# Two norm tiles transposed by transfers, and a filter transposed by column-tiled products, in a fused mixer kernel

## The chip, the cores and the metric

The kernel runs on one core of a Trainium2 chip. The core's engines run side by side: TensorE (PE in the profile, with PEld for its weight loads), VectorE (DVE), ScalarE (ACT), GpSimd (POOL) and SyncE (SP), which here issues nearly all transfers (DMAs). The metric is the device time of one execution in microseconds; of a kernel, the median over its executions.

## The reference

Rows are 2048 tokens of 640 channels; all inputs are bfloat16. The result is `g*a + (1-g)*b`, with `g = sigmoid(sum(q*gate_w))` for each token.

- Branch a: `k` passes through a causal filter of 4 taps, `kv = k_shift * v`, and `kv` is convolved along the tokens with a filter of 2048 taps per channel (`ssm_k`), by Fourier transforms of length 4096; then `y + kv*ssm_D`, times `q`.
- Branch b, a mixer: `h = gelu(layernorm(x) @ w1)`, the four quarters of whose channels are shifted by 1, -1, 2 and -2 tokens, then `x1 = x + shifted @ w2`, and `x1 + gelu(layernorm(x1) @ w3) @ w4`, with `x = q`.

## The kernel before

The tokens lie in 16 *slots* of 128 (`s` below, one partition for each token). The convolution is done as a Fourier transform written as matrix products, in four steps. Step 1 (`s1h` for the filter, `s1x` for `kv`) multiplies each slot's 128x640 block by cosines and sines (`TRIG`), step 2 (`s2h`, `s2x`) transforms along the slots, `pa`/`pb` multiply the two spectra on VectorE, `s3` and `s4` transform back. Between the steps the data go to DRAM and come back in another layout: `wF` writes step 1's result, `rF` reads it, `wG` and `rG` do the same behind `s3`.

Names used below, with their lines in the profile: `st1`, `rs1`, `nm1` are statistics and normalisation of the first layer norm (L577 to L631); `tr1` transposes two normalised slots on TensorE (L609) and `ev1`/`evh` copy them from PSUM to `xnT` (L387 on ScalarE, L389 on VectorE; `evh` makes the two wrapped-around slots at either end). `w1` is the product with w1 (L689, L693 for its 32-column tail), `w2` that with w2 (L715), `x1` adds it to x (L722). `w3`, `w4` (L817, L833, L842) are the second half of the mixer. `kv` (L878, L882, L886) is the chain of 32 VectorE operations for `k_shift * v`. `fo` (L1051) writes the last output rows.

The filter comes in channel-major (`SK`, 128 channels x 2048 taps, five blocks) and must be turned to tap-major (`HT`). `trh` (L859) does one block by 16 TensorE transposes of 128x128, whose stationary operand is every 16th tap of `SK`, into one bf16 PSUM pair of banks; `evt` copies the 128x2048 result out. That puts the two token halves `g` on alternating partitions, so step 1 of the filter (L911) contracts over all 128 partitions with a matrix `BM` in which every other row is zero: `BM` is cleared by GpSimd (`bz`, L499) and filled by two transfers from `TRIG` (`bm`, L503). Step 1 of `kv` (L913) has the halves in partitions 0 to 63 and 64 to 127, and multiplies each half in its own 64x128 tile of TensorE.

The order of all work is a list of task numbers, `ORDER`, each with a letter for its engine; every engine does its tasks in that order, whatever is ready. A planner (`Plan.place`) walks the list with a duration for each task and fixes which buffer each task takes. It also decides how many *fill* products (L255: products of a zero tile with no use, to keep TensorE running while it waits in the first microseconds) stand in front of each task. The fills read the zero tile `FZ`, which the task `zeros` (L506) clears on VectorE. Semaphores come from the real dependences; the planner's times do not enter the program.

TensorE's order before, up to step 2 (cN.. are groups of four slots; a mode other than 128x128 in brackets):

```
fill gwm trh.1 sgm tr1.4 trh.2 trh.4 tr1.0 trh.3 tr1.2 tr1.14 w1.0.3 w1.0.0 w1.0.2 w1.0.1 trh.0 w1.1.2
s1h.4 s1hr.4 tr1.6 s1h.0 w1.0.4[128x32] tr1.8 w1.1.0 s1h.7 s1h.6 s1h.5 w1.1.1 w1.1.4[128x32] s1hr.0 s1h.3
w1.1.3 w2.3 w2.1 s1h.1 w2.2 w2.0 w2.4 s1h.2 tr1.10 w2.6 s1h.8 s1h.10 w2.5 s1h.11 w2.7 tr1.12 w1.2.2 s1hr.8
s1h.9 w1.2.0 s1h.12 w1.2.4[128x32] w1.2.3 s1h.15 s1h.13 w1.3.2 w1.3.1 s1hr.12 w1.3.3 s1h.14 w1.2.1 w1.3.4[128x32]
w1.3.0 w2.10 w2.9 (then s1x[64x128] in eleven runs among w2, gate and w3.0) s1x.1 s1x.3 w4.2 w4.1 w4.0 w4.3
s2h.0.0 ...
```

36 fills are issued: 5 before `fill`, 6 before `gwm`, 14 before `tr1.4`, 11 in the gaps behind. On SP stand in order, from the 11th on: `ldsk3 ldw1 ldx6 ldsk0 bm ldx10 wCJ ldk15 ldk11 rCJ ldw2b3 ldw2a ldw2b1 ldw2b0 ldw2b2 ldkh1 wFh.4 ldk7 ldv3 ldk3 wFh.0 ldw3 ldkh0 ldv2 wFh.8.1 dt2.0`. `ldkN` and `rCJ` bring `k` and the four taps, without which `kv` can't start; `dt2` are transfers that transpose the second norm's rows. `wCJ` writes out the taps that GpSimd has rearranged (`cjp`). No more than eight transfers are in flight: the ninth waits for the first.

Of the kernel before, what the change touches and what calls it, by code (L numbers as in the profile page):

```python
# [83 lines left out]
class Plan:  # L84
# [13 lines left out]
    def add(self, name, eng, dur, fn, r=(), w=(), use=(), acq=(), rel=(), roles=(), after=(), mode=None, nbytes=0):  # L98
# [3 lines left out]
        t.kept = None  # L102
        t.acq = [(a, 1, a == "U") if isinstance(a, str) else a for a in acq]
# [13 lines left out]

    def close(self):
        by_role = {}
# [27 lines left out]
    def place(self, order):  # L147
# [6 lines left out]
        mode, bw, flying, self.kept = None, 0.0, [], None  # L154
        start, end = [None] * n, [None] * n
        for i in order:
# [34 lines left out]
            else:  # L191
                d = t.dur
# [17 lines left out]
                free[e] = end[i] = at + d  # L210
            for (o, p, k) in t.rel:
# [143 lines left out]
def build(env, nc, io):  # L355
    pl = Plan()
    add = pl.add
    for name, n in (("U", 8), ("xn", 4), ("hs", 2), ("x1nT0", 1), ("x1nT1", 1), ("h2", 2), ("FS", 2), ("FX", 5), ("XS", 2), ("HS", 2), ("PP", 2),
                    ("GX", 4), ("Q", 2), ("O", 2), ("V", 4)):
        pl.pool(name, n)  # L360
# [50 lines left out]
    add("ident", "POOL", 0.55, c_id, r=["iotb"], w=["ID"])  # L411
# [86 lines left out]
    BM = lambda: env.early("BM", [P, 2, 2048], BF16)  # L498
    add("bz", "POOL", 1.9, lambda t: nc.gpsimd.memset(BM().rearrange("p g q -> p (g q)").bitcast(F32), 0.0), r=["ID"], w=["BM"], roles=("C0",))  # L499
# [4 lines left out]
    add("bm", "SP", 1.08, c_bm, r=["TRIG"], w=["BM"], nbytes=P * 4096 * HALF, roles=("C0",))  # L504

# [6 lines left out]
    add("cjp", {"POOL": 3.2, "ACT": 2.3}, 0, lambda t: copy(t, env["VC"][0:1, 3, :, :],  # L512
# [104 lines left out]
    DMA1 = ()  # L617
    pairs = [2, 4, 6, 8, 0, 14, 10, 12]
    for s0 in pairs:
        nm = []  # L620
        for s in (s0, s0 + 1):
            st1[s] = add(f"st1.{s}", {"DVE": 1.26, "ACT": 1.73}, 0, lambda t, s=s: f_st1(t, s), r=[("x", s, 0), ("x", s, 1)],
                         w=[("MV", s)])
            add(f"rs1.{s}", "POOL", 0.85, lambda t, s=s: f_rs1(t, s), r=[("MV", s), "c0"], w=[("RS", s)])
        for s in (s0, s0 + 1):
# [7 lines left out]
            nm1[s] = add(f"nm1.{s}", {"DVE": 0.445, "ACT": 1.2}, 0, f_nm1, r=[("RS", s), ("x", s, 0), ("x", s, 1)],  # L633
# [10 lines left out]
        def f_ev1(t, s0=s0, tt=tt):  # L644
            copy(t, env["xnT"][:, s0 + 2:s0 + 4, :, :], tview(env.Ub(tt.buf["U"][0])))
        add(f"ev1.{s0}", {"ACT": 1.25, "DVE": 0.82}, 0, f_ev1, use=[tt], rel=[(tt, "U")], w=[("xnT", s0), ("xnT", s0 + 1)],
            roles=("xnT",))
        if s0 in (14, 0):
            h0 = 0 if s0 == 14 else 18

            def f_evh(t, s0=s0, tt=tt, h0=h0):
# [10 lines left out]
            add(f"evh.{s0}", {"DVE": 1.0, "ACT": 1.3}, 0, f_evh, use=[tt], rel=[(tt, "U")], w=[("xnT", a), ("xnT", a + 1)],  # L662
                roles=("xnT",))
# [130 lines left out]
    for c in range(4):  # L794
        nT, nP = None, f"x1nT{c % 2}"
        for s0 in (4 * c, 4 * c + 2):
            ss = (s0, s0 + 1)
            add(f"ve2.{s0}", {"DVE": 0.42, "POOL": 1.5}, 0, lambda t, s0=s0: f_ve2(t, s0), r=[("x", s, 0) for s in ss] + [("S2", s) for s in ss],
# [308 lines left out]
```

## Time and profile before

| | us |
|---|---|
| median of 3 executions (224.55 to 225.7) | 225.08 |
| the profiled execution, its own time | 227.05 |
| its span, first to last event | 225.3 |
| TensorE busy | 212.7 |
| VectorE busy | 189.3 |
| ScalarE busy | 154.4 |
| GpSimd busy | 45.8 |

Busy time counts fills as well as work. Rows of windows give, for one stretch, its length, then the busy time of each engine with its number of instructions in brackets (PE, PEld, DVE, ACT, POOL), the granted TensorE clock (1.00 is full speed, and it was that throughout), the share of the 16 DMA engines that were busy, and GB/s. Rows of the chain give start, length and the work; rows of a timeline give start, length, engine, line, operation, tiles and count, and in square brackets the idle time before it and what ended it.

### The profile page before, as it was taken

The page shows a single profiled execution, that of the slowest core. Times are in us where ns is not written, and L with a number is a line of the kernel's source. Part 1 is how long each engine was busy: PE and PEld are TensorE (multiplying, and loading weights), DVE is VectorE, ACT ScalarE, POOL GpSimd, SP SyncE. Part 2 cuts the span into 40 slices and gives each one's busy share as a digit, 9 for nine tenths or more (in the row PEclk, how much of TensorE's full clock was granted, in tenths as well). Part 3 has the DMA queues.
Part 4 walks back from the last instruction along what each step waited for, and adds up shares of the span by engine and source line. Part 5 has one row for each costly group of instructions (what it writes and reads, how often), then busy time and mean ns, then how long its engine had stood idle before and what let it go on. Part 6 is the DMA issues. An engine that isn't in the chain of part 4 may idle for free.

```text
span 225.3 us, 5381 instructions
## 1 busy us (share of the span) xinstructions
PE 212.7 (94%) x2161; PEld 106.4 (47%) x2178; DVE 189.3 (84%) x281; ACT 154.4 (69%) x225; POOL 45.8 (20%) x86
## 2 busy tenths in 40 slices
PE   3999889899999999999999999999999999999992
PEld 1576454466444444345543433334444555555561
DVE  7998896999999999997469989899857426989984
ACT  6998969799988999889658988888675002225000
POOL 7481532436200009930710000000000000000000
PEclk9999999999999999999999999999999999999999
DMA  6999999999999998979899989999992596988624
GB/s 193 281 308 232 220 237 238 327 233 327 349 240 287 241 272 252 379 270 270 193 367 311 373 154 285 316 304 309 247 255 88 185 374 209 281 250 249 203 64 116
DMA packets 39503, 57.94 MB, mean 257 GB/s; under 512 B 15027, under 2 KB 30645, under 8 KB 39478
## 3 DMA queue, kind: packets, MB, share of 16 engines
q1 hardware_dynamic: 39158, 57.27, 89.9%
q10 hardware_dynamic: 320, 0.33, 0.5%
q8 instruction: 17, 0.28, 0.5%
q14 instruction: 8, 0.07, 0.1%
HBM read 35.56 MB, written 18.36 MB: 239 GB/s over the span
## 4 chain that ended last, share of the span: by engine, by line
PE 63%; DMA 17%; DVE 12%; SPq 3%; issue 2%; ACT 1%; DVEq 0%
PE PS L817 18%; PE PS L833 17%; PE PS L715 9%; DMA x<-in_A_q_dram 7%; PE PS L965 5%; DMA W<-in_B_w_dram 4%; PE PS L689 4%; PE PS L993 4%; DMA SK<-in_A_ssm_k_dram 3%; DVE VC L878 3%; DVE VC L882 3%; DMA QO<-in_A_q_dram 2%; SPq L382 2%; PE PS L911 2%; PE PS L1031 1%
## 5 line engine op out<-in xcount | busy, mean ns | idle before, releaser
L824 ACT ACTIVATE h2T<-PS 128x512 bf16<-128x512 f32 x48 | 27.9, 605 | 27.3 <-PE PS L817 26.9
L833 PE MATMUL PS<-W,h2T 128*128 128x512 bf16 (+3 forms) x306 | 39.8, 298 | 0.3
L387 ACT CAST FS<-PS 128x1024 bf16<-128x1024 f32 x37 | 36.0, 1021 | 5.4 <-PE PS L913 3.5
L817 PEld LDWEIGHTS <-W 128*128 128x128 bf16 (+1 forms) x300 | 22.1, 103 | 29.4 <-issue 8.4
L833 PEld LDWEIGHTS <-h2T 128*128 128x128 bf16 (+1 forms) x312 | 22.4, 100 | 18.5 <-issue 1.6
L387 ACT CAST XH<-PS 128x1024 bf16<-128x1024 f32 x26 | 25.5, 1020 | 7.5 <-PE PS L965 7.4
L817 PE MATMUL PS<-x1nT,W 128*128 128x512 bf16 x120 | 28.5, 380 | 0.0
L817 PE MATMUL PS<-XB,W 128*64 128x512 bf16 (+1 forms) x180 | 28.5, 380 | 0.0
L980 DVE TENSOR_TENSOR PP<-XH 128x2048 bf16<-128x2048 bf16 x20 | 23.6, 1219 | 3.1 <-ACT XH L387 2.8
L878 DVE TENSOR_TENSOR VC<-K,VC 128x2560 bf16<-128x2560 bf16 x16 | 23.7, 1490 | 2.3 <-DMA W<-in_B_w_dram 2.1
L715 PE MATMUL PS<-W,hsT 128*128 128x128 bf16 (+1 forms) x155 | 23.5, 297 | 0.9 <-DMA W<-in_B_w_dram 0.6
L850 DVE TENSOR_TENSOR x<-PS,x 128x640 bf16<-128x640 f32 x12 | 9.8, 823 | 13.4 <-PE PS L833 13.2
L689 PE MATMUL PS<-xnT,W 128*128 128x512 bf16 x80 | 19.2, 379 | 0.1
L715 PEld LDWEIGHTS <-hsT 128*128 128x128 bf16 x160 | 12.8, 98 | 13.0 <-issue 1.1
L882 DVE TENSOR_TENSOR VC<-VC 128x2560 bf16<-128x2560 bf16 x12 | 17.9, 1489 | 0.3
L389 DVE CAST XH<-PS 128x1024 bf16<-128x1024 f32 x14 | 16.9, 1220 | 1.2 <-PE PS L965 1.1
L1037 DVE SCALAR_TENSOR_TENSOR W<-PS,GG,QO 128x640 bf16<-128x640 f32 x16 | 13.6, 877 | 2.4 <-PE PS L1031 1.9
L387 ACT CAST GS<-PS 128x1024 bf16<-128x1024 f32 x12 | 12.0, 1016 | 3.9 <-PE PS L993 3.9
L255 PE MATMUL PS<-C 128*128 128x512 bf16 x34 | 9.9, 434 | 3.8 <-DVE C L506 3.7
L842 PE MATMUL PS<-W,h2T 128*64 128x512 bf16 (+1 forms) x192 | 13.4, 299 | 0.0
L722 DVE SCALAR_TENSOR_TENSOR x<-PS,x 128x640 bf16<-128x640 f32 x16 | 12.8, 815 | 0.1
L965 PE MATMUL PS<-FX,TRIG 64*32 64x512 bf16 x320 | 12.4, 381 | 0.3 <-ACT GS L387 0.3
(115 smaller groups left out, 294.0 us busy)
## 6 DMA issues: line engine op xcount, KB each, us to landing
FH<-FS SPq DMA_DIRECT2D x8, 640.0 KB, 6.3
FXD<-FS SPq DMA_DIRECT2D x8, 640.0 KB, 5.0
FX<-FH SPq DMA_DIRECT2D x10, 512.0 KB, 6.0
FX<-FXD SPq DMA_DIRECT2D x10, 512.0 KB, 5.3
GX<-GD SPq DMA_DIRECT2D x8, 640.0 KB, 5.9
W<-in_B_w_dram SPq DMA_DIRECT2D x2, 1920.0 KB, 11.9
GD<-GS SPq DMA_DIRECT2D x8, 480.0 KB, 4.0
SK<-in_A_ssm_k_dram SPq DMA_DIRECT2D x5, 512.0 KB, 6.5
```

Of the source, the lines that this page charges most:

```text
L387: nc.scalar.copy(out=out, in_=in_)
L389: (nc.vector if t.on == "DVE" else nc.gpsimd).tensor_copy(out=out, in_=in_)
L689: nc.tensor.matmul(m[:, b, :], lhsT=W[:, 0, kb, 160 * fb:160 * fb + 128], rhs=rhs(kb, shifts[fb]), start=(kb == 0), stop=(kb == 4))
L715: nc.tensor.matmul(m[:, c0:c1], lhsT=env["hsT"][:, o.buf["hs"][0], fb, 128 * (s % 4):128 * (s % 4) + 128], rhs=env["W12"][:, 1, fb, c0:c1] ...
L817: nc.tensor.matmul(env.PS[q:q + w, t.buf["U"][0], :], lhsT=env["W3"][:, kb, 128 * fb + q:128 * fb + q + w], rhs=env.nT(int(nP[-1]))[:, :, ...
L824: nc.scalar.activation(out=env["h2T"][:, o.buf["h2"][0], fb, :], in_=env.PS[:, t.buf["U"][0], :], func=ACT.Gelu_apprx_tanh)
L833: nc.tensor.matmul(m[q:q + w, c0:c1], lhsT=env["h2T"][:, o.buf["h2"][0], fb, a:a + w], rhs=env["W4"][:, fb, c0:c1], start=(fb == 0), stop= ...
L878: nc.vector.tensor_tensor(out=VC[:, o], in0=env["K"][:, a + 3 - j:a + 7 - j, :], in1=w, op=ALU.mult)
L882: nc.vector.tensor_tensor(out=VC[:, 1], in0=VC[:, 1], in1=VC[:, 2], op=ALU.add)
L965: nc.tensor.matmul(env.U(t.buf["U"][0])[32 * j:32 * j + 32, gp, :], lhsT=CRI()[64 * gp:64 * gp + 64, 32 * pc:32 * pc + 32], rhs=X[64 * gp: ...
L980: nc.vector.tensor_tensor(out=env["PP"][:, o.buf["PP"][0], a, :].rearrange("p (b c) -> p b c", b=2), in0=X.unsqueeze(1).broadcast_to([P, 2 ...
L1037: nc.vector.scalar_tensor_tensor(out=u, in0=env.Uf(t.buf["U"][0])[:, 0:D], scalar=SS("GG")[:, s:s + 1], in1=env["QO"][:, 2 * q.buf["Q"][0] ...
```

## The change

1. **Slots 10 to 13 of the first norm.** `tr1.10`, `tr1.12` and their copies `ev1.10`, `ev1.12` go. Four transposing transfers `dt1.10` to `dt1.13`, issued by SP, bring the rows from `xn` to `xnT`.
2. **The filter's transposes.** Each of five blocks of 16 transposes becomes two tasks of 16 plain products with the identity, in 128x64 tiles: the stationary operand is 64 columns of `SK`, taps 32 apart, for one half `g`; the result is f32, so one pair of banks holds half a block. The ten copies `evt.cb.h` take 128x1024 each. The halves now lie in partitions 0 to 63 and 64 to 127.
3. **The filter's step 1** uses the same 64x128 products as `kv`'s. `BM`, the clearing `bz` and the transfers `bm` go.
4. **A new order, new durations and new rules for the planner.** Its durations for several small tasks are changed; it now models VectorE operations that wait for two GpSimd tasks, and keeps `ev1` and `evh` of slots 0 and 14 from running at once. None of these is an instruction of its own. All of `ORDER` is replaced: the engine of some tasks (`evt` seven times on ScalarE and three times on VectorE, for two and three before), and the place of nearly all.

TensorE's new order up to step 2:

```
fill tr1.14 tr1.2 tr1.4 tr1.0 gwm w1.0.3 w1.0.0 w1.1.2 trh.4.0[128x64] w1.0.4[128x32] w1.0.2 trh.2.0[128x64] w1.0.1
(128x64:) trh.2.1 trh.4.1 trh.1.0 trh.0.0 (f:) tr1.6 (128x64:) trh.3.0 trh.3.1 (f:) tr1.8 (128x64:) trh.0.1 trh.1.1
(64x128:) s1h.4 (f:) w1.1.0 w1.1.1 (64x128:) s1h.7 s1h.5 s1h.6 w1.1.4[128x32] (f:) w1.1.3 (64x128:) s1hr.4 (f:) w2.2 w2.3
(64x128:) s1h.0 s1hr.0 (f:) w2.0 w2.5 (64x128:) s1h.3 (f:) w2.1 (64x128:) s1h.1 s1h.2 (f:) w2.7 w1.2.2 w2.4
(64x128:) s1h.8 s1h.9 (f:) w2.6 w1.2.0 (64x128:) s1hr.8 s1h.10 s1h.11 (f:) w1.2.1 sgm w1.2.4[128x32] w1.2.3
(64x128:) s1h.12 s1h.14 gate[128x32] (f:) w1.3.2 w2.11 w1.3.1 (64x128:) s1h.15 (f:) w1.3.3 w2.8 w2.9
(64x128:) s1h.13 s1hr.12 s1x.12 (f:) w2.10 ... w3.0.0 ... s1x.0 s1x.3 s1xr.0 w2.13 s1x.1 s1x.2 w4.0 w4.2 w4.1 w4.3 s2h.0.0
```

(f: 128x128.) Along the whole list TensorE changes its tiling 113 times, for 84 before; up to step 2, 56 times for 32. 40 fills are issued: 12 before `fill`, 20 before `tr1.14`, 2 before `tr1.2`, 6 before `tr1.4`. On VectorE `zeros` now stands behind the first statistics: `warm0 kz phase1 phand phsmall st1.15 zeros gwz st1.3 ...`. SP's new list begins `ldx14 ldx2 ldx4 ldx0 ldx6 ldgw ldw1 ldCJ ldx10 ldsk4 ldsk2 wCJ ldsk1 ldsk3 ldsk0 ldk15 ldk11 rCJ ldw2b1 ldw2b0 ldw2b2 ldD ldw2a ldw2b3 dt1.11 dt1.10 ldk7 ldv3 dt1.12 wFh.4 ldkh1 dt1.13 wFh.0 ldk3 dt2.0 ldv2 wFh.8 dt2.1 ldw3`.

```diff
-    DMA1 = ()
+    DMA1 = (10, 12)
...
-    BM = lambda: env.early("BM", [P, 2, 2048], BF16)
-    add("bz", "POOL", 1.9, lambda t: nc.gpsimd.memset(BM().rearrange("p g q -> p (g q)").bitcast(F32), 0.0), ...)
-    def c_bm(t):
-        for g in range(2):
-            nc.sync.dma_start(out=BM()[g::2, g, :], in_=env["TRIG"][64 * g:64 * g + 64, 0:2048])
...
-    for cb in range(5):
-            sk = env["SK"][:, cb, :].rearrange("c (q s) -> c q s", s=16)
-            o = env.Ub(t.buf["U"][0])
-            for i in range(16):
-                nc.tensor.transpose(o[:, 128 * i:128 * i + 128], sk[:, :, i], env["ID"][:])
-        t = add(f"trh.{cb}", "PE", 1.0, trh, ..., mode="f", roles=("SK",))
-        add(f"evt.{cb}", {"ACT": 1.86, "DVE": 1.23}, ...)
+    for cb, h in [(cb, h) for cb in range(5) for h in range(2)]:
+            sk = env["SK"][:, cb, :].rearrange("c (n g s) -> c g n s", g=2, s=16)
+            o = env.Uf(t.buf["U"][0])
+            for i in range(8):
+                for g in range(2):
+                    nc.tensor.matmul(o[64 * g:64 * g + 64, 128 * i:128 * i + 128], lhsT=sk[:, g, :, 8 * h + i], rhs=env["ID"][:],
+                                     start=True, stop=True)
+        t = add(f"trh.{cb}.{h}", "PE", 0.5, trh, ..., mode="c64", roles=("SK",))
+        add(f"evt.{cb}.{h}", {"ACT": 1.03, "DVE": 1.23}, ...)
...
         def prod(out, s, c0, c1, g):
-            if which == "h":
-                nc.tensor.matmul(out, lhsT=BM()[:, g, 128 * s:128 * s + 128], rhs=src(s)[:, c0:c1], start=True, stop=True)
-            else:
-                nc.tensor.matmul(out, lhsT=B()[64 * g:64 * g + 64, s, :], rhs=src(s)[64 * g:64 * g + 64, c0:c1], ...)
-        mode, dur, durr = ("f", 0.44, 0.47) if which == "h" else ("r64", 0.23, 0.28)
+            nc.tensor.matmul(out, lhsT=B()[64 * g:64 * g + 64, s, :], rhs=src(s)[64 * g:64 * g + 64, c0:c1], start=True, stop=True)
+        mode, dur, durr = "r64", 0.23, 0.28
```

The branch that `DMA1` switches on stands in the kernel before, unused: for each slot one `nc.sync.dma_start_transpose(out=env["xnT"][:, s + 2, :, :], in_=env["xn"][:, n.buf["xn"][0], :])`, behind the slot's `nm1`.

More of the change, by code (lines that the diff above doesn't have):

```diff
@@ L116, in add @@
         return t
+    LOCKS = ("nm1.", "nm2.", "kv", "pa.", "pb.", "pc.", "ad.", "ax.", "phase1", "phand", "phsmall")
     def close(self):
+        for t in self.tasks:
+            t.lock, t.hold = t.name.startswith(self.LOCKS), t.name in ("cjp", "dfold")
         by_role = {}
@@ L191, in place @@
             else:
+                if t.lock and e == "DVE" and held[0] <= at < held[1]:
+                    start[i] = at = held[1]
                 d = t.dur
@@ L210, in place @@
                 free[e] = end[i] = at + d
+                if t.hold and e == "POOL":
+                    held = (at, end[i])
             for (o, p, k) in t.rel:
@@ L511, in build @@
                                                   in_=io["sk"].rearrange("d j -> (d j)").unsqueeze(0)), w=["CJR"], roles=("VC",))
-    add("cjp", {"POOL": 3.2, "ACT": 2.3}, 0, lambda t: copy(t, env["VC"][0:1, 3, :, :],
+    add("cjp", {"POOL": 2.6, "ACT": 2.3}, 0, lambda t: copy(t, env["VC"][0:1, 3, :, :],
                                                             env["VC"][0:1, 2, :, :].rearrange("p a b -> p (a b)").rearrange("p (d j) -> p j d", j=4)),
@@ L621, in build @@
         for s in (s0, s0 + 1):
-            st1[s] = add(f"st1.{s}", {"DVE": 1.26, "ACT": 1.73}, 0, lambda t, s=s: f_st1(t, s), r=[("x", s, 0), ("x", s, 1)],
+            st1[s] = add(f"st1.{s}", {"DVE": 1.37, "ACT": 1.7}, 0, lambda t, s=s: f_st1(t, s), r=[("x", s, 0), ("x", s, 1)],
                          w=[("MV", s)])
@@ L645, in f_ev1 @@
             copy(t, env["xnT"][:, s0 + 2:s0 + 4, :, :], tview(env.Ub(tt.buf["U"][0])))
-        add(f"ev1.{s0}", {"ACT": 1.25, "DVE": 0.82}, 0, f_ev1, use=[tt], rel=[(tt, "U")], w=[("xnT", s0), ("xnT", s0 + 1)],
-            roles=("xnT",))
+        e1 = add(f"ev1.{s0}", {"ACT": 1.25, "DVE": 0.82}, 0, f_ev1, use=[tt], rel=[(tt, "U")], w=[("xnT", s0), ("xnT", s0 + 1)],
+                 roles=("xnT",), acq=(f"T{s0}",) if s0 in (14, 0) else ())
         if s0 in (14, 0):
@@ L661, in build @@
             a = -2 if s0 == 14 else 16
-            add(f"evh.{s0}", {"DVE": 1.0, "ACT": 1.3}, 0, f_evh, use=[tt], rel=[(tt, "U")], w=[("xnT", a), ("xnT", a + 1)],
-                roles=("xnT",))
+            eh = add(f"evh.{s0}", {"DVE": 0.9, "ACT": 1.3}, 0, f_evh, use=[tt], rel=[(tt, "U")], w=[("xnT", a), ("xnT", a + 1)],
+                     roles=("xnT",), acq=(f"T{s0}",))
+            for o in (e1, eh):
+                o.rel.append((o, f"T{s0}", None))
             add(f"evz.{s0}", {"POOL": 0.15, "DVE": 0.07}, 0, lambda t, z=(0, h0) if s0 == 14 else (127, h0):
```

58 lines of the change are left out of this document (17 added, 41 removed), and 5 rows, old and new, of the table ORDER.

## The prediction

> **What bounds the kernel now.** I read the page's first part, then windows cut where the work changes hands, then the chain of waits.
>
> ```profile
> PE 212.7 (94%) x2161; PEld 106.4 (47%) x2178; DVE 189.3 (84%) x281; ACT 154.4 (69%) x225; POOL 45.8 (20%) x86
> ...
> 20.00:40.63 20.63, 17.88 (x149) 8.88 (x148) 16.53 (x40) 17.43 (x29) 6.13 (x11) 1.00 1.00 240
> 40.63:101.33 60.70, 60.16 (x434) 29.10 (x442) 59.44 (x72) 53.55 (x81) 22.02 (x27) 1.00 1.01 287
> 101.33:114.47 13.14, 13.09 (x103) 7.36 (x112) 7.17 (x16) 9.18 (x19) 5.01 (x15) 1.00 0.97 251
> 114.47:206.50 92.03, 91.34 (x1138) 41.93 (x1144) 73.62 (x77) 55.97 (x73) 0.00 (x0) 1.00 0.91 267
> 206.50:225.30 18.80, 14.36 (x212) 8.85 (x208) 14.47 (x21) 0.60 (x1) 0.00 (x0) 1.00 0.49 139
> ```
>
> From 40.63 us, the first `w2`, TensorE is idle for only 1.3 us until 206.50. So the end is set by three things: when TensorE can begin without gaps, how much it has to do, and whether VectorE keeps pace. VectorE matters because between 40.63 and 101.33 it is busy for 59.44 of 60.70 us too. The transfers are a third limit: the DMA share is 1.00 in the head.
>
> ```profile
> 48.45 0.56 PE PS L609 x10
> ...
> 50.37 0.86 PE PS L911 x4
> 51.23 1.36 PE PS L715 x10
> ...
> 63.81 0.45 PE PS L911 x8
> ...
> 71.94 0.54 PE PS L913 x4
> ...
> 73.94 0.32 PE PS L913 x2
> 74.27 1.46 PE PS L715 x10
> 75.73 0.55 PE PS L913 x10
> ...
> 96.30 1.49 DVE K L886
> ...
> 101.33 6.84 PE PS L833 x49
> ...
> 114.47 0.56 PE PS L965 x16
> ```
>
> In the chain, the `kv` stretch on VectorE ends at 96.30 + 1.49 = 97.79; step 1 of `kv` ends at 101.33; four `w4` fill the wait for the round trip through DRAM; step 2 starts at 114.47, 16.7 us behind the end of `kv`. So two paths meet at 114.47, TensorE's own work and VectorE's `kv`, and I follow both.
>
> **TensorE's work, from those rows.** A pair of filter products costs 0.86/2 = 0.43 us in 128x128 and, by the `kv` rows, 0.54 - 0.32 = 0.22 in 64x128. The tails of four slots cost 0.45 and 0.55 - 0.32 = 0.23. A block in 64x128 pays for its two changes of tiling, though: one pair alone takes 0.32, and the `w2` behind it 1.46 where it otherwise takes 1.36. That is 0.10 in and 0.10 out, so a filter pair standing alone (0.32 + 0.10) saves nothing against 0.43; only pairs put together do.
>
> In the stretch from `w2` to the last `s1x`, the old list has ten pairs and two tails (4.3 + 0.9) and `tr1.10`, `tr1.12` (2 x 0.56): 6.3 us. The new one has twelve pairs, three tails and `sgm` (2.64 + 0.69 + 0.1): 3.4. Counted along the two lists, changes of tiling in this stretch go from 27 to 38, + 1.1. Net 60.16 - 6.3 + 3.4 + 1.1 = 58.4, and 58.9 with the old idle time: 1.8 us less. From step 2 on, the list has 57 changes for 52: 0.5 us more, with nothing removed there.
>
> **The transposes of the filter.** Which price a 128x64 product has is the open one.
>
> ```profile
> 14.33 1.17 PE L859 MATMUL PS<-ID,SK 128*128 128x128 bf16 x16
> 15.33 0.81 PE L255 MATMUL PS<-C 128*128 128x512 bf16 x3
> ...
> 212.84 8.03 PE L842 MATMUL PS<-W,h2T 128*64 128x128 bf16 x144
> ```
>
> Sixteen old transposes take 15.33 - 14.33 = 1.00 us, 62 ns each, where the norm's transposes with closely packed weights take 0.56/10 = 56: the strided weights cost 6 ns each. The last row holds 24 pairs of 512 columns (24 x 0.216 = 5.2) and 48 pairs of 128 in 128x64 tiles: (8.03 - 0.15 for the last one's tail - 5.2)/48 = 56 ns a pair. So a new task of eight pairs takes 0.45 us if its weights keep pace, ten tasks 4.5 for the old 5.0. It takes 1.0 if a strided load of 64 columns takes as long as one of 128 (16 x 62 ns): 10 us in all. The low end is a row of this tiling with packed weights, the high end a row of these weights in another tiling. I take 0.5, since a load half as wide at the old cost per column takes 31 ns, 62 a pair.
>
> [...]
>
> **The head.**
>
> ```profile
> 3.73 4.12 PE L255 MATMUL PS<-C 128*128 128x512 bf16 x11 [3.73 <-DVE C L506]
> ...
> 8.88 3.19 PE L255 MATMUL PS<-C 128*128 128x512 bf16 x14
> ...
> 20.34 4.48 PE L689 MATMUL PS<-xnT,W 128*128 128x512 bf16 x20
> ...
> 40.63 2.89 PE L715 MATMUL PS<-W,hsT 128*128 128x512 bf16 x19 [0.59 <-DMA W<-in_B_w_dram]
> ...
> 6.49 0.68 DVE L577 BATCH_NORM_STATS2 BS<-x 128x6 f32<-128x512 bf16 x1
> ...
> 18.74 2.50 DVE L389 COPY xnT<-PS 128x1280 bf16<-128x1280 bf16 x4
> ...
> 31.78 0.68 DVE L577 BATCH_NORM_STATS2 BS<-x 128x6 f32<-128x512 bf16 x1
> ...
> 33.06 0.81 DVE L389 COPY xnT<-PS 128x1280 bf16<-128x1280 bf16 x1
> ...
> 35.07 1.32 DVE L631 TENSOR_SCALAR xn<-x,SA,RS 128x640 bf16<-128x640 bf16 x3
> ...
> 38.45 2.89 DVE L878 TENSOR_TENSOR VC<-K,VC 128x2560 bf16<-128x2560 bf16 x2 [2.06 <-DMA W<-in_B_w_dram]
> ...
> 42.79 0.81 DVE L722 SCALAR_TENSOR_TENSOR x<-PS,x 128x640 bf16<-128x640 f32 x1
> ...
> 99.31 0.44 DVE L603 TENSOR_SCALAR xn<-x,r,SB 128x640 bf16<-128x640 bf16 x1
> ...
> L389 DVE COPY HT<-PS 128x2048 bf16<-128x2048 bf16 x3 | 3.7, 1221 | 0.7 <-PE PS L859 0.7
> L387 ACT CAST FS<-PS 128x1024 bf16<-128x1024 f32 x37 | 36.0, 1021 | 5.4 <-PE PS L913 3.5 <-PE PS L911 1.6 <-PE PS L689 0.2
> ...
> C<-TRIG SPq DMA_DIRECT2D x2, 256.0 KB
> W<-in_B_w_dram SPq DMA_DIRECT2D x2, 1920.0 KB, 11.9
> x1nT<-xn SPq DMA_TRANSPOSE x8, 5.8
> ```
>
> The fills waited for the zero tile (3.73, released by L506). The new list clears it behind the first `st1`. That one started at 6.49, behind 0.9 us of small clears and masks that now come later, so it starts at 5.6; with 1.28 for itself (33.06 - 31.78) and the clear, the first fill runs at 7.1 us. 32 fills stand ahead of `tr1.14`: eleven at the starting rate (4.12 us less a tail of 0.15) and 21 at (3.19 - 0.15)/14 = 0.22 make 8.6, so `tr1.14` runs at 15.7, some 3.5 us after its rows are normalised. Behind it come 0.56, two fills, `tr1.2`, six fills, `tr1.4` and its copy: the first `w1` starts at 20.1, where it was 20.34. The reordered loads of x gain nothing here.
>
> VectorE then has, from 19.2: four `ev1` (3.0) and `evh` (0.9), by the 2.50 us row; `gwc` 0.4; five `st1` of 1.28; seven `nm1` of 0.44; three `evt` of 1.22. Sum 17.5: `kv` can start at 36.7, and I take 37.0 since `nm1` operations overlap GpSimd's `dfold`. Before, it started at 38.45, after a wait for transfers. Those come sooner: `bm` moved 2 x 256 KB ahead of the taps and k, 2.2 us at 240 GB/s. SP waits at `wCJ` for GpSimd's `cjp`, though, with seven queued loads behind, and may lose as much; I put the taps at 35 to 36.5.
>
> TensorE from 20.1: six `w1` (five of 1.1, one of 1.3) and seven tasks `trh` with their changes to 30; `tr1.6`, `tr1.8` and three `trh` to 33.6; `s1h.4`, four `w1`, the three pairs and `s1hr.4` to 40.1. W2, which ended the last wait at 40.63, should land by 38.5 to 40.5. So `w2` starts at 40.1. ScalarE has 3.2 us free in 20.63 and takes five more `evt`, of 1.02, and three `ev1` fewer: covered, just.
>
> The transposing transfers: `w1.2` needs them, on the new list some 12 to 20 us behind the first `w2`, and they are issued at 35 to 45 with 5.8 us to land: covered. On SP each passes in front of `ldk7`, `ldv3` or `wFh`; VectorE needs those at 48 us and later. If that cover fails, each us comes off the `kv` path.
>
> **The sum.** TensorE's path: 40.1 + 58.9 + 13.14 = 112.1. VectorE's path: the old stretch is 97.79 - 38.45 = 59.34; now one `x1` (0.8) and one `nm2` (0.45) stand behind it, and `gz` (97.79 to 99.31: 1.5) and `sg` (0.15) in it: 59.7, to 96.7. Behind it two pairs, a tail, `w2.13`, two pairs, with changes: 2.8, then 13.14: 112.6. Before, it took 16.7, with `gz` in between. The later one, 112.6, is 1.9 before 114.47. Less 0.5 for the later changes of tiling: 1.4 us. The last part keeps its form: VectorE's `fo` behind the last `w4`, loads of q before them.
>
> The profiled execution took 227.05, of which the span is 225.3; it gives 225.65. It stands 1.97 above the median, so against the median: 225.08 - 1.4 = 223.7.
>
> **Rivals.** *Slower: strided weights set the pace of `trh`.* At 1.0 us a task, 5 us more than I took lie on TensorE between 20 and 40 us, where after 20.1 it has no gap to spare: `w2` starts at 45.1, step 2 at 45.1 + 58.9 + 13.14 = 117.1, 2.7 later than before, and the end is 228.3. It decides from about 0.65 us a task, where the gain is gone; the measured 62 ns speak for it, the 56 ns pairs against.
>
> *No change: W3 comes late.* `ldw3` moves behind `dt2.1` on SP, which waits for ScalarE's `nm2.1` (about 61 us); 11.9 us for so large a load gives 74 to 75, and `w3.0.0`, earlier on the new list, wants it at 76. Two us of delay there, or as much lost by other waits of the new order, puts the end at 224 to 226.
>
> *More: the fills don't delay.* If `tr1.14` runs at 12 us, `kv` starts with the taps at 35.2 and `w2` with W2 at 38.7; step 2 starts at 110.8, and the end is 221.9. Against it: the fills are in the instruction stream and can't be skipped.
>
> **How the numbers follow.** Small gain 0.34, of which 0.08 stays within half a per cent; more 0.14; no change 0.22, of which 0.03 ends slower; slower 0.30. The likeliest gives 223.7 (its own range 222.6 to 224.6). To leave out two in ten, the range goes from 221.5, below the larger gain, to 228.5, the slower rival. About 0.5% (1.1 us) is what a measurement can tell; by it 0.40 faster (0.34 - 0.08 + 0.14), 0.27 same, 0.33 slower.
>
> **What would show it.** L859 in 128x64 with 16 products in about 0.5 us (or 1.0); L913-like filter pairs at 0.22; the first fill at 7.1 and `tr1.14` near 15.7; `kv`'s first product near 37; the first `w2` near 40; step 2 near 112.6, then 92 to 93 us to the last `w3`. A longer wait of TensorE at `w3.0.0`, or idle time above 2 us between 40 and 206, makes the forecast wrong.

## The result, and the profile after

The kernel became slower: 233.63 us median of 5 executions (232.62 to 236.11), beside 225.01 for the kernel before. The ratio is 1.0382, 95% interval 1.0334 to 1.043. The forecast was 223.7 us with a range of 221.5 to 228.5: wrong in sign and outside the range. The profiled execution took 232.62 us, of which the span is 230.8.

The page's first part, and the windows of the changed kernel, cut at the first `w1`, the first `w2`, the end of `kv`'s step 1, step 2, and in the last part. The columns are those of the windows above. Two cuts differ from the prediction's: its first window starts at 20.00, 0.34 us ahead of the first `w1`, and its last cut is the end of the last `w3`, which in the changed kernel comes at 208.97, while 212.80 is the end of the `w4` products behind it.

```profile
PE 216.1 (94%) x2242; PEld 107.7 (47%) x2242; DVE 187.4 (81%) x276; ACT 155.9 (68%) x229; POOL 41.2 (18%) x89
...
20.63:45.78 25.15, 24.06 (x276) 15.31 (x276) 19.70 (x46) 20.55 (x30) 5.97 (x11) 1.00 0.75 188
45.78:106.46 60.68, 58.51 (x437) 26.51 (x434) 56.93 (x69) 53.63 (x79) 17.88 (x24) 1.00 1.03 294
106.46:119.61 13.15, 13.15 (x99) 7.38 (x98) 7.62 (x15) 9.29 (x20) 5.95 (x18) 1.00 1.10 250
119.61:212.80 93.19, 92.61 (x1146) 42.75 (x1144) 74.73 (x77) 57.23 (x76) 0.00 (x0) 1.00 0.92 266
212.80:230.80 18.00, 14.32 (x210) 8.82 (x208) 12.90 (x19) 0.00 (x0) 0.00 (x0) 0.98 0.48 142
```

The loss is in the first row. From the first `w1` to the first `w2` TensorE now takes 25.15 us and is busy for 24.06 of them; before, the same stretch took 40.63 - 20.34 = 20.29. The next two stretches have the lengths they had, and from step 2 to the end it is 111.19 us for 110.83. The timeline of TensorE shows what fills that row (L237 fills, L583 `tr1`, L665 `w1`, L836 `trh`, L691 `w2`, L888 step 1, L940 step 2):

```profile
6.94 9.37 PE L237 MATMUL PS<-C 128*128 128x512 bf16 x32 [6.94 <-DVE C L480]
16.15 0.72 PE L583 MATMUL PS<-ID,xn 128*128 128x128 bf16 x10
...
20.63 2.32 PE L665 MATMUL PS<-xnT,W 128*128 128x512 bf16 x10 [0.25 <-DVE xnT L371]
24.04 1.24 PE L665 MATMUL PS<-xnT,W 128*128 128x512 bf16 x5 [1.09 <-ACT hsT L682]
...
28.63 1.11 PE L836 MATMUL PS<-ID,SK 128*64 128x128 bf16 x16
...
30.85 3.78 PE L836 MATMUL PS<-ID,SK 128*64 128x128 bf16 x64
34.57 0.73 PE L583 MATMUL PS<-ID,xn 128*128 128x128 bf16 x10
...
45.78 2.89 PE L691 MATMUL PS<-W,hsT 128*128 128x512 bf16 x20
...
103.70 0.83 PE L888 MATMUL PS<-K,TRIG 64*128 64x512 bf16 x12 [1.04 <-DVE K L864]
...
119.61 0.63 PE L940 MATMUL PS<-FX,TRIG 64*32 64x512 bf16 x16
```

Four `trh` in a row start at 30.85, and the work behind them at 34.57: 0.93 us each, where the forecast had 0.5. VectorE pays too (L371 `evt`, L856 and L864 the first and last operation of a `kv` group):

```profile
33.84 1.23 DVE L371 CAST HT<-PS 128x1024 bf16<-128x1024 f32 x1 [3.56 <-PE PS L836]
...
41.33 2.88 DVE L856 TENSOR_TENSOR VC<-K,VC 128x2560 bf16<-128x2560 bf16 x2
...
89.32 1.49 DVE L864 TENSOR_TENSOR K<-VC 128x2560 bf16<-128x2560 bf16 x1 [1.32 <-DMA VC<-in_A_v_dram]
...
102.15 1.49 DVE L864 TENSOR_TENSOR K<-VC 128x2560 bf16<-128x2560 bf16 x1
```

It stands idle 3.56 us for the slow `trh`, starts `kv` at 41.33 instead of 37.0, and ends it at 102.15 + 1.49 = 103.64.

### The profile page after: what moved, and what is told of

It reads as the page before. It is cut to its first block, busy times and chain, and to the rows that moved or that the text cites. A ratio compares the mean times of both kernels' runs of the same rounds, so it can differ in the third digit from the quotient of the medians.

```text
span 230.8 us, 5544 instructions
## 1 busy us (share of the span) xinstructions
PE 216.1 (94%) x2242; PEld 107.7 (47%) x2242; DVE 187.4 (81%) x276; ACT 155.9 (68%) x229; POOL 41.2 (18%) x89
## 4 chain that ended last, share of the span: by engine, by line
PE 70%; DVE 8%; DMA 7%; ACT 7%; issue 4%; POOL 2%; SPq 0%; DVEq 0%; ACTq 0%
PE PS L793 18%; PE PS L809 14%; PE PS L691 7%; PE PS L818 6%; PE PS L665 5%; PE PS L940 5%; PE PS L968 4%; PE PS L836 4%; DMA x1nT<-xn 4%; DMA QO<-in_A_q_dram 3%; PE PS L888 3%; DVE VC L860 2%; DVE VC L856 2%; POOL RS L569 2%; PE PS L669 2%
## 5 line engine op out<-in xcount | busy, mean ns | idle before, releaser
L369 ACT CAST FS<-PS 128x1024 bf16<-128x1024 f32 x38 | 37.2, 1021 | 5.5 <-PE PS L888 4.2
L809 PE MATMUL PS<-W,h2T 128*128 128x128 bf16 (+3 forms) x312 | 40.5, 299 | 0.0
L793 PEld LDWEIGHTS <-W 128*128 128x128 bf16 (+1 forms) x300 | 22.5, 102 | 30.6 <-issue 10.1
L793 PE MATMUL PS<-XB,W 128*64 128x512 bf16 (+1 forms) x180 | 29.1, 380 | 0.6 <-DVE W L1012 0.6
L793 PE MATMUL PS<-x1nT,W 128*128 128x512 bf16 x120 | 28.3, 380 | 0.9 <-DMA x1nT<-xn 0.9
L369 ACT CAST XH<-PS 128x1024 bf16<-128x1024 f32 x25 | 24.7, 1014 | 6.3 <-PE PS L940 6.3
L691 PE MATMUL PS<-W,hsT 128*128 128x512 bf16 (+1 forms) x160 | 23.9, 299 | 0.2 <-DVE x L698 0.2
L856 DVE TENSOR_TENSOR VC<-K,VC 128x2560 bf16<-128x2560 bf16 x16 | 23.7, 1489 | 0.2
L665 PE MATMUL PS<-xnT,W 128*128 128x512 bf16 x80 | 19.6, 380 | 1.3 <-ACT hsT L682 1.1
L371 DVE CAST XH<-PS 128x1024 bf16<-128x1024 f32 x15 | 18.0, 1220 | 2.2 <-PE PS L940 1.3
L691 PEld LDWEIGHTS <-hsT 128*128 128x128 bf16 x160 | 12.9, 98 | 12.7 <-issue 1.6
L237 PE MATMUL PS<-C 128*128 128x512 bf16 x40 | 11.4, 448 | 6.9 <-DVE C L480 6.9
L761 POOL TENSOR_TENSOR r<-v,MH 128x2 f32<-128x2 f32 x8 | 10.9, 1369 | 24.1 <-DVE v L756 23.6
L369 ACT CAST GS<-PS 128x1024 bf16<-128x1024 f32 x13 | 12.8, 1015 | 2.9 <-PE PS L968 2.9
```

The costliest lines, as they stand in the source:

```text
L369: nc.scalar.copy(out=out, in_=in_)
L371: (nc.vector if t.on == "DVE" else nc.gpsimd).tensor_copy(out=out, in_=in_)
L665: nc.tensor.matmul(m[:, b, :], lhsT=W[:, 0, kb, 160 * fb:160 * fb + 128], rhs=rhs(kb, shifts[fb]), start=(kb == 0), stop=(kb == 4))
L691: nc.tensor.matmul(m[:, c0:c1], lhsT=env["hsT"][:, o.buf["hs"][0], fb, 128 * (s % 4):128 * (s % 4) + 128], rhs=env["W12"][:, 1, fb, c0:c1] ...
L793: nc.tensor.matmul(env.PS[q:q + w, t.buf["U"][0], :], lhsT=env["W3"][:, kb, 128 * fb + q:128 * fb + q + w], rhs=env.nT(int(nP[-1]))[:, :, ...
L809: nc.tensor.matmul(m[q:q + w, c0:c1], lhsT=env["h2T"][:, o.buf["h2"][0], fb, a:a + w], rhs=env["W4"][:, fb, c0:c1], start=(fb == 0), stop= ...
```

## The experiments

Times of the same events in the profiled executions (us), which the sections below refer to:

| kernel | first `w1` | `kv` starts | first `w2` | step 2 | span | median |
|---|---|---|---|---|---|---|
| before, the execution the prediction read | 20.34 | 38.45 | 40.63 | 114.40 | 225.3 | 225.01 |
| before, another execution (e14) | 20.55 | 35.71 | 38.69 | 112.45 | 222.8 | |
| forecast | 20.1 | 37.0 | 40.1 | 112.6 | 223.9 | 223.7 |
| after | 20.63 | 41.33 | 45.78 | 119.61 | 230.8 | 233.63 |
| after, packed columns (e1) | 20.57 | 38.65 | 41.81 | 116.44 | 227.4 | 228.99 |
| after, zero tile first (e5) | 19.42 | 40.08 | 44.53 | 118.57 | 229.1 | 230.93 |
| after, both (e11) | 19.43 | 36.51 | 40.42 | 114.03 | 224.7 | 227.78 |

The forecast's span is that of the execution read, 225.3, less 1.4.

### The same transposes from neighbouring columns

```diff
-  lhsT=sk[:, g, :, 8 * h + i]
+  lhsT=env["SK"][:, cb, 8 * h + i + 1024 * g:8 * h + i + 1024 * g + 64]
```

> The changed kernel with one thing different: the stationary operand of each filter transpose is 64 neighbouring taps of SK instead of 64 taps 32 apart, so the filter that comes out is in the wrong order (the values leave out the reference's filter order; every instruction count is the same). Theory A (strided loads of 64 columns set the pace of the transposes, 0.93 us a task, and everything behind them moves by that): a task takes 0.45 us, kv starts near 37 instead of 41.3, the first w2 near 41 instead of 45.8, step 2 near 115 instead of 119.6, and the time is 4 to 5 us below the changed kernel's 233.6, about 229. Theory B (the transposing transfers and the fills hold the head, the transposes are hidden): a task is shorter, but w2 stays later than 44 and the time above 232.

228.99 us, ratio 1.0172 (1.0116 to 1.0227): by the medians about 4.6 us of the 8.6 lost are the strides of the weights; in the two profiled executions step 2 comes 3.2 us sooner. Theory A has the time right, but `kv` starts at 38.65 and step 2 at 116.44, some 1.5 us later than it said. The groups of the transposing line, with the weight loads apart, first in the changed kernel, then with packed columns (the three durations are least, median and most, in ns):

```profile
L836 PEld LDWEIGHTS <-SK x160: 185/204/208, 25.2 to 39.5; 128*64 128x64 bf16 x160
```

```profile
L836 PEld LDWEIGHTS <-SK x160: 106/110/111, 25.1 to 35.3; 128*64 128x64 bf16 x160
```

The products are the same in number, shape and place in the order. They read other columns of the same tile, 64 neighbouring ones instead of 64 that lie 32 apart, so what they compute is not the filter; and the load takes 110 ns instead of 204. Four tasks in a row with packed columns:

```profile
29.80 1.98 PE L836 MATMUL PS<-ID,SK 128*64 128x128 bf16 x64
31.71 0.73 PE L583 MATMUL PS<-ID,xn 128*128 128x128 bf16 x10
```

A task takes (31.71 - 29.80)/4 = 0.48 us instead of 0.93. The forecast's 0.5 was right for packed weights only.

### At which stride the price rises

In the changed kernel each of the five blocks got its own stride (2 to 32 elements); in the kernel before, likewise for the 128-column transposes (1 to 16).

```diff
+  st = (2, 4, 8, 16, 32)[cb]     # after; before: (1, 2, 4, 8, 16)[cb]
-  lhsT=sk[:, g, :, 8 * h + i]
+  lhsT=env["SK"][:, cb, off(i, g):off(i, g) + 63 * st + 1:st]
```

> The changed kernel with a different stride of the 64-column loads in each of the five blocks of the filter: 2, 4, 8, 16 and 32 elements of bf16 (4 to 64 bytes); block 3 and 4 of the list keep their places. The filter's order is wrong on the first four. If the price comes from reading one column in each 16-byte line, strides of 8, 16 and 32 elements cost the same 58 ns a product and 2 and 4 cost less; if it grows with the distance, 8 lies between 28 and 58; if any stride costs the full price, 2 costs 58 too.

> The kernel before with a different stride of the 128-column loads in each of the five blocks of the filter: 1, 2, 4, 8 and 16 elements (the filter's order is wrong on the first four). [...] The time of the kernel stays within 1 us of 225.

233.87 us and 225.21 us, one execution each. Groups by form: busy us and mean ns of one load behind the bar. First 64 columns in 128x64 tiles, with steps of 2, 4, 8, 16 and 32 elements (two bytes each; the row for 16 holds both halves of its block):

```profile
L837 PEld LDWEIGHTS <-SK 128*64 128x64 bf16 x17 | 0.6, 112 | 0.1
...
L837 PEld LDWEIGHTS <-SK 128*64 128x64 bf16 x15 | 0.6, 145 | 0.2 <-issue 0.2
...
L837 PEld LDWEIGHTS <-SK 128*64 128x64 bf16 x16 | 1.0, 214 | 0.4 <-issue 0.4
...
L837 PEld LDWEIGHTS <-SK 128*64 128x64 bf16 x32 | 2.0, 216 | 0.1
...
L837 PEld LDWEIGHTS <-SK 128*64 128x64 bf16 x16 | 1.0, 203 | 0.4 <-issue 0.4
```

Then 128 columns in 128x128, with steps of 1, 4, 8 and 16:

```profile
L859 PEld LDWEIGHTS <-SK 128*128 128x128 bf16 x15 | 0.9, 98 | 0.1
...
L859 PEld LDWEIGHTS <-SK 128*128 128x128 bf16 x15 | 0.9, 114 | 0.1
...
L859 PEld LDWEIGHTS <-SK 128*128 128x128 bf16 x15 | 1.0, 147 | 0.4 <-issue 0.4
...
L859 PEld LDWEIGHTS <-SK 128*128 128x128 bf16 x15 | 1.0, 150 | 0.1
```

In both tilings the price stops rising at a step of 8 elements, which is 16 bytes. But full width pays 150 ns for 128 columns, and a product loses only some 7 ns by it (from the first of 16 transposes to the work behind them 0.89 us packed, 1.00 at step 16). In the 128x64 tile a load of half as many columns costs 203 to 216 ns, and a product goes from 30 ns to 58 (0.48/16 and 0.93/16). Even packed, 64 columns take 110 ns there, beside 98 for 128 in 128x128. So what fails is the step from the old cost per column to 0.5 us a task: that cost did not stay, but went from 150/128 = 1.2 ns to 204/64 = 3.2. Why the narrower load costs more, these rows don't show.

### The zero tile first

```diff
-  ORDER: warm0 kz phase1 phand phsmall st1.15 zeros ...
+  ORDER: warm0 zeros kz phase1 phand phsmall st1.15 ...
```

> The changed kernel with the clearing of the zero tile first on VectorE, as in the kernel before; the planner then puts 34 fills ahead of tr1.14, 3, 6 and 1 behind. Theory A says that TensorE is without a gap from the first w1 to w2, so what the fills held up is paid in full: tr1.14 near 12.5 instead of 16.2, the first w1 near 17.5 instead of 20.6, w2 near 43, the time about 3 us lower, 230 to 231. Theory B2 (kv on VectorE or the transfers set the end): less than 1 us.

230.93 us, ratio 1.0252 (1.0216 to 1.0288): 2.7 us less than the changed kernel by the medians; in the profiled executions step 2 comes 1.0 us sooner. In the timeline of TensorE the fills now start at 1.60 us, and the wait moves to the rows:

```profile
1.60 8.80 PE L237 MATMUL PS<-C 128*128 128x512 bf16 x33
...
18.51 0.45 PE L583 MATMUL PS<-ID,xn 128*128 128x128 bf16 x5 [1.28 <-DVE xn L605]
...
19.42 2.32 PE L665 MATMUL PS<-xnT,W 128*128 128x512 bf16 x10
```

The first `w1` comes at 19.42, 1.2 us sooner, not 3. `tr1.0` now waits 1.28 us for its normalised rows: behind the fills the norms were next.

### The transposing transfers, taken out of one kernel and put into the other

```diff
-    DMA1 = (10, 12)     # out of the changed kernel, with tr1.10, tr1.12 and their copies back
+    DMA1 = ()
```

> The changed kernel with slots 10 to 13 transposed on TensorE again (two tr1 among the w2, their copies on ScalarE), without the four transposing transfers. Theory A: SP no longer stands from 33 to 40 us, ldk7, ldv3 and the writes behind come sooner, but kv and w2 wait for the filter's transposes, so the end moves by less than 1.5 us either way (1.1 us of TensorE work comes back). Theory B (the transfers' place on SP starves the head): 3 to 5 us faster, w2 and kv sooner.

```diff
-    DMA1 = ()           # into the kernel before, its order else unchanged
+    DMA1 = (10, 12)
```

> The kernel before with only the first part of the change: slots 10 to 13 by transposing transfers in the places of tr1.10 and tr1.12 in the list. Theory A: 1.1 us of TensorE work goes from a stretch where VectorE keeps it company, so 0 to 1 us faster. Theory B: the transfers wait for nm1.10 on SP and hold what stands behind (ldw3, ldv2), 1 to 4 us slower.

Without them the changed kernel takes 233.54 us (1.0361, 1.0308 to 1.0414): no difference. So the saving of the 1.1 us that `tr1.10` and `tr1.12` take on TensorE, which the forecast counted, does not show in the time. With them alone the kernel before takes 230.4 (1.0233, 1.017 to 1.0295): some 5 us lost, more than the rival theory had. Timelines of TensorE and VectorE and a window of that second kernel (L666 `w1`'s tail, L859 there the last product of a `kv` group):

```profile
60.26 2.85 PE L666 MATMUL PS<-xnT,W 128*32 128x512 bf16 x19 [3.40 <-DMA xnT<-xn]
...
70.82 1.49 DVE L859 TENSOR_TENSOR K<-VC 128x2560 bf16<-128x2560 bf16 x1 [4.82 <-DMA VC<-in_A_v_dram]
...
60.00:65.00 5.00, 4.74 (x28) 1.64 (x29) 4.90 (x4) 2.52 (x5) 0.00 (x0) 0.66 1.02 338
```

`w1.2` comes too soon for them under the old order, and `ldv2`, queued behind them on SP, reaches VectorE 4.82 us late. This does not account for the whole loss: of the 5.6 us by which step 2 is later there than in e14 (118.04 and 112.45), 2.1 lie at the start of `kv` already (37.82, behind a wait of 1.46 us for `k`), and the first of the transfers goes out at 46.90, behind that. In the changed kernel SP waits for these rows as well, and the first transfer goes out at 40.31:

```profile
40.31 2.64 SPq L612 DMA_TRANSPOSE xnT<-xn  x2
```

But the last of the four goes out at 50.69 and `w1.2` starts at 55.83; in the kernel above two of them go out only at 53.35, and `w1.2`, in whose tail TensorE waits 3.40 us, stands sooner. The transfers are covered by the place that the new order gives them.

### Parts 2 and 3 under the old order

```diff
+  trh.cb -> trh.cb.0 trh.cb.1, evt.cb -> evt.cb.0 evt.cb.1   (changed tasks, the old ORDER and fills)
-  bz, bm
```

> The second and third part of the change (filter by 128x64 products, step 1 in 64x128, no BM) under the order of the kernel before, with its fills, and without the transposing transfers; the second half of each block is transposed behind the copy of the first. Theory A: 4.3 us more TensorE work in the transposes, 1 to 2 us of tiling changes, up to 4 us less in step 1, 2 us less of transfers: 225 to 229. If the new order is what costs, this run is at or below 225.

238.18 us, ratio 1.0555 (1.0502 to 1.0608): both theories missed. The old order has most `trh` in front of the first `w1`, in gaps of the head; twice as many tasks, each as long as an old one and with a copy of its own, don't fit there. The first `w1` starts at 29.40, the first `w2` at 51.93. Windows of it:

```profile
20.00:30.00 10.00, 8.89 (x78) 6.26 (x75) 4.58 (x8) 3.11 (x4) 0.00 (x0) 0.67 1.04 234
...
40.00:50.00 10.00, 10.00 (x94) 4.39 (x93) 9.08 (x21) 9.12 (x15) 2.23 (x5) 0.83 0.01 2
```

The granted clock fell to 0.67 and 0.83; under the changed kernel's order it was 1.00 from 20.63 to 212.80 us. So the new order is worth about 4.6 us to the new transposes (238.18 against 233.54 without the transfers); against the old one, it isn't what lost the time.

### Step 1 of the filter alone

```diff
-  if which == "h":  nc.tensor.matmul(out, lhsT=BM()[:, g, ...], rhs=src(s)[:, c0:c1], ...)
+  nc.tensor.matmul(out, lhsT=B()[64 * g:64 * g + 64, s, :], rhs=src(s)[64 * g:64 * g + 64, c0:c1], ...)
-  bz, bm: clear and load BM
```

> The kernel before with only step 1 of the filter in 64x128 tiles, BM neither cleared nor loaded; the halves stay on alternating partitions, so the filter's spectrum is not the reference's (this part of the values is left out). Its own worth: transfers 0.5 MB less ahead of kv (up to 2 us sooner), TensorE less by 0.2 us for each filter pair that stands together and nothing for one alone. Theory A: 1 to 2.5 us faster than before. Rival (VectorE's kv or the transfers behind it bound the stretch, and nothing comes through): within 0.5 us.

224.3 us, ratio 0.994 (0.9911 to 0.9968): 1.3 us faster than the kernel before. In its timeline step 2 starts 0.7 us sooner than in e14:

```profile
111.73 0.62 PE L962 MATMUL PS<-FX,TRIG 64*32 64x512 bf16 x16
```

So the 64x128 products, together with the clearing and the loads of `BM` that they spare, are a gain; how much each of the two gives isn't shown. What the change pays for the layout that they need is several times as much.

### Both repairs, and one load moved on SP

```diff
-  lhsT=sk[:, g, :, 8 * h + i]                              # e11, e12: packed columns, as in e1
-  ORDER: ... phsmall st1.15 zeros ...                      # e11, e12, e13: zeros behind warm0, as in e5
-  SP: ... dt2.3 dt2.2 wFh.12.1 wFh.12.0 ldv1 ...           # e12, e13
+  SP: ... dt2.3 ldv1 dt2.2 wFh.12.1 wFh.12.0 ...
```

> The changed kernel with both edits that won time alone: the ten transposing tasks read 64 neighbouring columns (the filter's taps then stand in another order, which is left wrong), and the zero tile is cleared first, with 44 fills in front of the first real products. Measured alone they gave 4.6 and 2.7 us. Theory A (two stretches in a row on one path): the gains add up, 226.3 us, 225.6 to 227.4, a ratio to before of about 1.006; kv starts at 36.0 to 37.2 us, step 2 at 113.5 to 114.5 us. Theory B (the transposes were slow partly since they came late, on top of other work on VectorE, or one gain hides the other): 228 us or more, kv at 38 us or later.

> The kernel of the run before this one (packed columns, zero tile first; filter order wrong), and the load ldv1 issued on SP before dt2.2 instead of behind it and the two wFh.12. With packed columns alone, VectorE waited 1.38 us for ldv1, which SP issued at 76.44 us behind a transfer that held SP for 7.44 us. Theory A (the rest of the miss is that wait): the wait is gone and 0.8 to 1.4 us with it, 225.0 us (224.3 to 226.0), no slower than the kernel before by more than 0.5%. Theory B (something else is late there next, step 1 of the last slots or the loads for step 2): the wait goes and the time stays within 0.5 us of the run before this one.

> The changed kernel with its strided transposes as they are (nothing left out), the zero tile cleared first and ldv1 issued before dt2.2. Theory A: 2.7 us for the zero tile, as measured alone, and 0.8 to 1.4 us for the load: 229.7 us (229.0 to 230.6), a ratio to before of about 1.02, the rest being the strided weights. Theory B (ldv1's wait of 1.32 us in the changed kernel is there since VectorE's chain, being late, finds the load in a crowd of other transfers): no gain beside the zero tile's, 230.9 us.

Both repairs together give 227.78 us, ratio 1.012 (1.0057 to 1.0183). The time is between the two theories; `kv` at 36.51 and step 2 at 114.03 are as theory A had them. By the medians the second repair is worth 1.2 us once the first is made (228.99 to 227.78), where it was worth 2.7 alone, but step 2 comes 2.4 us sooner, where it came 1.0 sooner alone. The four executions range from 226.52 to 229.09, so these runs don't tell 1.2 from 2.7. Its timelines:

```profile
36.51 2.88 DVE L856 TENSOR_TENSOR VC<-K,VC 128x2560 bf16<-128x2560 bf16 x2
...
40.42 2.89 PE L691 MATMUL PS<-W,hsT 128*128 128x512 bf16 x19
...
114.03 0.63 PE L940 MATMUL PS<-FX,TRIG 64*32 64x512 bf16 x16
```

The moved load was a mistake: 231.87 us (1.0298, 1.025 to 1.0346), 4 us worse than without the move, and 236.13 (1.0474, 1.0428 to 1.0521) with the strided weights, 5 us worse than e5. VectorE's wait for `ldv1` did go, as theory A had it. But the transposing transfer behind it, `dt2.2`, came late, and TensorE waited for it; just ahead of the operation that needs `ldv1`, VectorE then stood idle 4.82 us for `w2`. Of e12, SP's timeline, one step of its chain, TensorE's timeline and a window; then TensorE of e13 (L793 is `w3`):

```profile
69.44 1.17 SPq L364 DMA_DIRECT2D VC<-in_A_v_dram  x2
70.66 1.41 SPq L784 DMA_TRANSPOSE x1nT<-xn  x1
...
70.66 9.81 DMA x1nT<-xn
...
80.56 4.42 PE L793 MATMUL PS<-x1nT,W 128*128 128x512 bf16 x10 [4.03 <-DMA x1nT<-xn]
...
80.00:85.00 5.00, 4.42 (x10) 1.61 (x12) 2.42 (x2) 0.00 (x0) 2.65 (x3) 0.50 1.07 361
```

```profile
85.24 3.97 PE L793 MATMUL PS<-x1nT,W 128*128 128x512 bf16 x10 [5.16 <-DMA x1nT<-xn]
```

SP issued `dt2.2` at 70.66 us, right behind the load's 640 KB, and it landed 9.81 us later; in e11, where the load went out behind it, `w3` could start at 76.73. The loss has two parts: 4.03 us of waiting, and behind it ten `w3` products that take 4.42 us, in a window with a clock of 0.50, where the changed kernel's ten take 2.32 (at 82.23, behind a wait of 0.89).

### The kernel before once more

No edit.

> The kernel before, unchanged, in one more profiled execution; it leaves nothing out. The execution that the prediction read took 227.05 us, 1.97 above the median, and its VectorE waited 2.06 us for a transfer in front of kv (start at 38.45 us, step 2 at 114.4, span 225.3). With the filter's transposes read at other strides (a change worth 0.3 us in all) the same program took 225.21 us, waited 0.29 us there, started kv at 36.53 and step 2 at 113.22. Theory A (that wait belongs to the one execution, not to the kernel): if this execution takes 224.3 to 225.8 us, its wait in front of kv is under 0.8 us, kv starts at 36.3 to 37.2, step 2 at 112.9 to 113.7, the span is 222.5 to 224.0; the prediction then credited the change with a gain that an ordinary execution of the kernel before has already. Theory B (the wait is the kernel's; the strides in that other run took it away): the wait is 1.5 us or more, kv starts after 38 us, and the 2 us between this execution and the one read lie elsewhere.

224.65 us, span 222.8. VectorE and TensorE:

```profile
35.71 2.89 DVE L878 TENSOR_TENSOR VC<-K,VC 128x2560 bf16<-128x2560 bf16 x2
...
38.69 2.88 PE L715 MATMUL PS<-W,hsT 128*128 128x512 bf16 x19
...
112.45 0.62 PE L965 MATMUL PS<-FX,TRIG 64*32 64x512 bf16 x16
```

Theory A, and further than it went: no wait in front of `kv` and none in front of `w2`. The waits that the prediction read (2.06 and 0.59 us, both put down to loads of weights) are not the kernel's own. In executions with the same order in the head, the wait in front of `kv` was 2.06 us (the one read), 1.46 (e7), 0.29 (e4) and 0 (this one).

## Why the prediction was wrong, point by point

The miss is 9.9 us, 223.7 to 233.63, and it splits by the table and the rows above. `kv` started at 41.33 for 37.0: 4.3 us. The `kv` stretch took 103.64 - 41.33 = 62.3 for 59.7: 2.6. From the end of `kv` to step 2 it took 15.97 where the forecast had 112.6 - 96.7 = 15.9, and from step 2 to the end 111.2 where 110.8 + 0.5 was foretold. (Within that last part the forecast had 92 to 93 us to the last `w3`; it took 208.97 - 119.61 = 89.4, with more `w4` behind it.) That is 6.9 in the profiled executions. The other 3.0 lie in how each stands to its median: 1.97 above (taken off by the prediction), and 1.0 below for the changed kernel.

- **The step that failed first: "I take 0.5".** The task `trh` measured 0.93, and packing its weights again gave 4.6 us back (e1). The prediction's bounds, 0.45 and 1.0, held the truth at their far end, and the reason for the choice ("a load half as wide at the old cost per column") was false: 64 columns in 128x64 cost more (203 to 216 ns) than 128 in 128x128 did (147 to 150). It explains most of the late `w2`: 40.1, and 4.3 for ten tasks, 0.5 for the later first `w1`, 1.1 for its wait for ScalarE before the third group (24.04 in the timeline) give 46.0; measured 45.78. It doesn't explain all of the 4.3 us at `kv`: with packed columns alone `kv` starts at 38.65, still 1.65 behind the forecast, and VectorE waits 1.22 and 0.20 us there for `trh`, where the forecast had added up its work without waits. That packed columns and an early zero tile together came to 40.42 and 36.51, close to the 40.1 and 37.0, is in part luck, since the first `w1` then starts 0.7 sooner than foretold.
- **The second: "so against the median: 225.08 - 1.4".** The profiled execution was 1.97 above the median, and it held the very wait that the change was credited with ending (38.45 to 37.0). The execution without that wait (e14) starts `kv` at 35.71 and step 2 at 112.45, 2 us sooner, so the forecast's 112.6 was no gain beside it. With `trh` at 0.5 and everything else as foretold, a sound forecast was a time about 0.6 us above that of e14 (0.15 at step 2, 0.5 behind it), not 1.4 below the median.
- **The third: "59.7" for the `kv` stretch.** It was worked out as the old stretch with single operations added and taken off; the old one had one wait in it, of 0.40 us. The rows show 1.32 us for `ldv1` and 1.1 us in three waits of `x1` for `w2` (0.16, 0.52 and 0.41). In the runs with the load moved, the first wait went at the price of a late transposing transfer, so it could not be won that way.
- **Right: the head's fills.** First fill at 6.94 (7.1 foretold), `tr1.14` at 16.15 (15.7), first `w1` at 20.63 (20.1). The rival "the fills don't delay" is refuted by this timeline and by e5: the late zero tile costs 2.7 us by the medians and 1.0 at step 2 alone, 1.2 and 2.4 with packed columns, so its price is known only as some 1 to 3 us.
- **Right: the filter's step 1.** TensorE's work between the first `w2` and the last `s1x` was put at 58.4; the window has 58.51. Alone, with `BM` gone, it gains 1.3 us (e10). In the changed kernel it buys nothing, since `kv` on VectorE ends the stretch (the 1.04 us wait at 103.70).
- **Right, on its condition: the transfers.** Covered in the changed kernel, but without the gain that the sum counted for them (e6). The prediction said what would happen if the cover failed, and under the old order it did (e7).
- **The rivals.** The one that came true is "strided weights set the pace", given 0.30. Its cause and its price (1.0 a task, for 0.93 measured) were right; its 228.3 us was too low by the second and third point and by the 1.0 us by which the changed kernel's profiled execution lies below its median. "W3 comes late" did not happen: `w3.0.0` waited 0.89 us, for `x1nT`.

What stays open: 2.7 us between both repairs (ratio 1.012) and the kernel before. The profiled executions e11 and e14 differ by 1.9: `kv` starts 0.8 later, its stretch is 1.4 longer (with 1.11 us of waiting for `ldv1`), 0.65 is made up behind it, and 0.3 come behind step 2. Whether another order of SP's queue would win them was tried with one load only. A layout that puts the halves in place with 128x128 transposes was not tried.

## What to carry to other kernels

These transposes use the data as weights, so the data's stride is paid in the weight load: 98 ns packed and 150 at the real stride for 128 columns in 128x128, 110 and 204 for 64 in 128x64. Before going to a narrower tile, compare load times at the real stride, in that tile. Price an unknown by the row that shares the property in doubt (here the strided weights, a task of 1.0 us, not the tiling, 0.45), and when a measured row speaks for the dear end, don't settle at the cheap one. When the profiled execution stands above the median, look for the wait that makes it so, and don't credit the change with ending it; a second profile of the same kernel shows whether the wait is always there.

## What the runs showed of the hardware

- A weight load of 128 columns in a 128x128 tile took 98 ns packed, 147 from columns 16 bytes apart and 150 from columns 32 bytes apart (e4). One of 64 columns in 128x64 took 110 ns packed (e1), and 214, 216 and 203 from columns 16, 32 and 64 bytes apart (e3).
- A gap of 3.40 us on TensorE was followed by a granted clock of 0.66 from 60 to 65 us (e7), one of 4.03 us by 0.50 from 80 to 85 (e12). In e8 TensorE had no gap above 1.4 us between 20 and 60 us; it was busy for 8.89 of the 10 us from 20 to 30 at a clock of 0.67 and for all of the 10 from 40 to 50 at 0.83. What sets the clock, these runs don't tell.
- A transposing transfer of one slot, issued directly behind a load of 640 KB, landed 9.81 us after its issue (e12); one step of order on SP cost 4 us of the whole (227.78 us in e11, 231.87 in e12).
